# Value sums of an attention kernel in two runs per batch instead of three, under a new order of work

## Chip, cores and metric

The kernel runs on one core of a Trainium2 chip. The metric is the device time of one execution in microseconds (us), as the median of several runs. PE is the matrix engine (TensorE), DVE the vector engine, ACT the scalar engine, POOL GpSimd, SP the engine that issues most transfers.

## What is computed

Four batches (b = 0 to 3) of 1088 rows go through two blocks. The first is a linear attention with polynomial features, whose output is the input `x` of the second, an attention in which every row uses two of four experts:

```python
kv = np.einsum('bhsf,bhsd->bhfd', k_p, v)          # k_p, q_p: 64 features per head of k and q
num = np.einsum('bhsf,bhfd->bhsd', q_p, kv)        # block 1: x = num / den
logits = x @ w_gate                                # block 2: two experts per row
topk = np.argpartition(-logits, K, axis=-1)[..., :K]
for e in range(E):
    scores = scale * (q @ k.transpose(0, 2, 1))    # q, k, v = x @ wq[e], x @ wk[e], x @ wv[e]
    scores = np.where(causal, -1000000000.0, scores)
    a = softmax(scores)                            # row maximum, exp, division by the sum
    ye = a @ v @ wo[e]
    out += mask[..., None] * w[:, :, kk:kk + 1] * ye   # for each of the row's two choices kk
```

Everything is 32-bit floating point. `wq[e] @ wk[e].T` and `wv[e] @ wo[e]` are multiplied out once (`Mq`, `Mo`), so that the scores are taken against `x` itself and the "values" that are summed are rows of `x`.

## The kernel before

The 1088 rows of a batch are 17 **tiles** of 64 rows; each tile has 128 partitions, since each row appears once per chosen expert. The tiles lie in three **groups**: 0 to 5, 6 to 11, 12 to 16. The work is written as some 1290 **jobs**, each a short piece for one engine, with what it reads, makes and holds. A table of numbers, `ORDER`, says in which order they are recorded, and so in which order each engine, which runs its own queue in order, meets them; a letter behind a number picks one of two engines for a job, or, for an idle matmul, whether it is there (`a`) or not (`b`). Buffers come from pools, and a job's first use of one takes the one longest free.

For each batch the jobs are, by the names used below:

- **Block 1**: load k, q, v; `turn k`, `turn q` (DVE transpositions), `sketch` (PE, L524), `back` (DVE, L527, transposes the sketch out of PSUM), `features` (DVE or POOL, L532), `sums` (PE, L576: features of k against v), `numer` (PE, L635 and L771), `divide`, `turn x`, `keep x`, which give `xT`.
- **Choice of experts**: `logits` (PE, L829 and L822), `turn logits`, `choose`, masks `mb`. The gate's weights are a small transfer of their own (`load w4`, `wgr`), which POOL spreads (`gate order`, L294).
- **Per group**: `query` (PE, L1018: two pairs of products with `Mq`), `base` (copies) and `pick` (DVE, L1031, a predicated copy by the masks), which give `qs`.
- **Per tile**: `score` (PE, L1056), `take` (DVE, L1068: mask, minimum), `exp` (ACT, L1084), `guard`, `invert` (DVE, L1095), `weigh` (POOL, L1099), `turn A` (DVE, L1104: the weighed scores transposed, 32 by 32, into the buffer `AT`).
- **Per group**: the value sum `sum b.n` (PE, L1132) over all of the group's key blocks, `keep V` (copies by ACT or DVE), `patch V` (DVE, L1162), `spread V` (POOL, L1166), and `out` (PE, L1260, L1210 for the group of five tiles). The very last group of the kernel (batch 3, group 0) uses `mix V` (DVE, L1171) and `scale V` (POOL, L1175), and its `out` goes expert by expert (L1236).

A **value sum** walks over blocks j of 32 keys, `J = 2*t1` of them for a group that ends at tile `t1`. Each j has four matmuls (32 contracted rows each, in the four 32-row quarters of the array) that run side by side. They have 32 columns for each tile that sees these keys, so at most 192 for a group of six and 160 for one of five, and fewer, in steps of 32, on the group's own diagonal. The first matmul of a sum can start only when `turn A` of all tiles of its group is done. Its results lie in two of the four PSUM **pairs** (a pair is two banks of 512 columns) until `keep V` and `patch V` have read them.

PSUM has those four pairs for everything: scores, queries, sketches, sums, outputs. `AT` has two buffers, used in turn by the groups of all batches (12 group sums in the kernel). At the start PE also runs "dummy" matmuls on zeros (`idle`, L251), which nobody reads.

## Time and profile before

| | |
|---|---|
| median of 3 runs | 259.52 us (259.01 to 259.92) |
| span of the profiled execution | 258.5 us |
| difference of median and span (start and end of the program around it) | 1.0 us |
| PE busy | 249.4 us, 96% |
| DVE busy | 207.2 us, 80% |
| POOL busy | 157.8 us, 61% |
| ACT busy | 108.0 us, 42% |

The time of the profiled execution as such is not given apart from its span; sums are made against the span, and the 1.0 us is added at the end. "Busy" for PE is generous: matmuls are pipelined, and a short pause between two of them is hidden in the modelled end of the first. The pieces of the chain of waits, which follow each other without a gap, tell better what PE spent.

### The profile page before, as it was taken

How to read it: one execution, taken by the hardware profiler on the slowest of the kernel's cores; microseconds unless marked ns; L12 is line 12 of the kernel's file. 1: busy time of each engine (PE TensorE's matmuls, PEld its weight loads, DVE VectorE, ACT ScalarE, POOL GpSimd, SP SyncE). 2: the span in 40 equal slices, each digit the busy share in tenths (PEclk: the TensorE clock that was granted, in tenths of full speed). 3: DMA queues.
4: the chain of work that ended last, by engine and by line, in shares of the span. 5: the costliest groups of instructions: out<-in, count | busy, mean ns of one | idle time of the engine just before them, and what ended most of it. 6: DMA issues, size and time to landing. Idle time of an engine off the chain costs nothing.

```text
span 258.5 us, 9931 instructions
## 1 busy us (share of the span) xinstructions
PE 249.4 (96%) x4159; PEld 185.6 (72%) x4161; DVE 207.2 (80%) x527; ACT 108.0 (42%) x287; POOL 157.8 (61%) x265
## 2 busy tenths in 40 slices
PE   7888998999999999999999999999999999999995
PEld 2467654576598896665799776765896975789994
DVE  6969899998987886999997387999888638878332
ACT  4346445872803505840634044624624316432110
POOL 6718489958489754577663976087366634533742
PEclk9999999999999999999999999999999999999999
DMA  6936379205827552702612694304252157430003
GB/s 212 240 98 174 92 195 252 45 3 127 215 54 147 126 146 79 193 3 82 172 32 38 125 249 126 84 18 140 42 90 76 53 136 184 110 60 3 3 4 86
DMA packets 40381, 27.88 MB, mean 108 GB/s; under 512 B 25872, under 2 KB 35600, under 8 KB 40336
## 3 DMA queue, kind: packets, MB, share of 16 engines
q1 hardware_dynamic: 39888, 26.62, 42.8%
q8 instruction: 32, 0.52, 0.9%
q10 hardware_dynamic: 448, 0.62, 0.7%
q14 instruction: 13, 0.11, 0.1%
HBM read 22.62 MB, written 4.62 MB: 105 GB/s over the span
## 4 chain that ended last, share of the span: by engine, by line
PE 83%; DMA 6%; DVE 5%; POOL 2%; issue 2%; ACTq 0%; ACT 0%; DVEq 0%; POOLq 0%
PE pair L1132 30%; PE pair L1056 26%; PE pair L1018 9%; PE pair L1260 7%; PE pair L1210 3%; DMA wgr<-in_moe_w_gate_dram 2%; DMA w<-in_v_dram 2%; PE pair L771 2%; POOL fp L532 2%; DMA in<-in_q_dram 2%; PE pair L524 1%; PE pair L576 1%; DVE qs L1031 1%; PE pair L1236 1%; PE pair L822 1%
## 5 line engine op out<-in xcount | busy, mean ns | idle before, releaser
L1099 POOL TENSOR_SCALAR w<-w,rs,sh 128x960 f32<-128x960 f32 (+15 forms) x68 | 56.5, 837 | 32.1 <-DVE rs L1095 29.5
L1056 PE MATMUL pair<-xT,qs 128*128 128x320 f32 (+11 forms) x216 | 73.7, 478 | 1.3 <-DVE rs L1095 0.7
L1084 ACT ACTIVATE w<-w,mx 128x768 f32<-128x768 f32 (+16 forms) x68 | 52.3, 769 | 48.0 <-DVE mx L1068 44.3
L1068 DVE CUSTOM_DVE_ANT_0 w<-pair,mask 128x192 f32<-128x192 f32 (+14 forms) x68 | 48.3, 723 | 11.3 <-PE pair L1056 9.1
L1056 PEld LDWEIGHTS pair<-xT,qs 128*128 128x128 f32 x216 | 38.3, 190 | 26.5 <-issue 10.9
L1104 DVE STREAM_TRANSPOSE AT<-w 128x64 f32<-128x64 f32 (+15 forms) x68 | 50.7, 758 | 4.6 <-POOL w L1099 4.5
L1132 PE MATMUL pair<-AT,xra 32*128 32x160 f32 (+5 forms) x1136 | 44.6, 302 | 0.0
L1132 PEld LDWEIGHTS pair<-AT,xra 32*128 32x128 f32 x1136 | 41.8, 185 | 3.7 <-issue 1.5
L1166 POOL TENSOR_TENSOR agg<-agg,mb 128x768 f32<-128x768 f32 (+1 forms) x22 | 33.9, 1557 | 13.0 <-ACT agg L194 8.8
L1018 PE MATMUL pair<-xT,Mq 128*128 128x384 f32 (+1 forms) x96 | 34.3, 477 | 0.1
L194 ACT COPY agg<-pair 128x384 f32<-128x384 f32 (+1 forms) x34 | 14.1, 464 | 48.4 <-PE pair L1132 45.5
L532 POOL TENSOR_TENSOR fp<-w 128x576 f32<-128x576 f32 x22 | 26.6, 1223 | 2.8 <-DVE w L527 1.8
L1132 PE MATMUL pair<-AT,xrb 32*128 32x160 f32 (+5 forms) x752 | 27.2, 288 | 0.0
L1132 PEld LDWEIGHTS pair<-AT,xrb 32*128 32x128 f32 x752 | 26.3, 185 | 0.8 <-issue 0.7
L1031 DVE COPY_PREDICATED qs<-mb,pair 128x768 f32<-128x768 uint16 (+1 forms) x24 | 23.1, 964 | 2.6 <-DMA mb<-me 1.2
L1018 PEld LDWEIGHTS pair<-xT,Mq 128*128 128x128 f32 x96 | 17.3, 190 | 10.0 <-issue 2.1
L1260 PEld LDWEIGHTS pair<-Mo,agg 128*128 128x128 f32 x168 | 20.6, 192 | 3.2 <-issue 1.4
L1260 PE MATMUL pair<-Mo,agg 128*128 128x128 f32 x168 | 21.3, 277 | 0.0
L1092 POOL TENSOR_SCALAR rs<-zs 128x1 f32<-128x1 f32 x28 | 6.3, 226 | 20.8 <-ACT w L1084 17.9
L1162 DVE COPY_PREDICATED agg<-mb,pair 128x384 f32<-128x384 uint16 (+1 forms) x24 | 12.8, 554 | 6.5 <-ACT agg L194 6.3
L194 ACT COPY qs<-pair 128x384 f32<-128x384 f32 (+1 forms) x18 | 7.8, 459 | 16.4 <-PE pair L1018 16.4
L527 DVE STREAM_TRANSPOSE w<-pair 128x576 f32<-128x576 f32 x16 | 11.6, 755 | 3.2 <-PE pair L524 3.0
(173 smaller groups left out, 288.6 us busy)
## 6 DMA issues: line engine op xcount, KB each, us to landing
xra<-xd SPq DMA_DIRECT2D x16, 192.0 KB, 4.6
xrb<-xd SPq DMA_DIRECT2D x16, 192.0 KB, 4.8
xrc<-xd SPq DMA_DIRECT2D x16, 160.0 KB, 4.6
in<-in_k_dram SPq DMA_DIRECT2D x7, 272.0 KB, 4.4
mb<-me SPq DMA_DIRECT2D x3, 576.0 KB, 6.1
mb<-me SPq DMA_DIRECT2D x6, 288.0 KB, 3.9
in<-in_q_dram SPq DMA_DIRECT2D x3, 544.0 KB, 6.4
xd<-w SPq DMA_DIRECT2D x12, 136.0 KB, 3.1
```

Source lines behind the costliest of these rows:

```text
L194: (nc.scalar.copy if eng == "ACT" else VEC[eng].tensor_copy)(o, i)
L532: VEC[e].tensor_tensor(out=f, in0=a[:, :, None, R : 2 * R].to_broadcast([128, NJ, R, R]), in1=a[:, :, 0:R, None].to_broadcast([128, NJ, R, ...
L1018: nc.tensor.matmul(plan[ps[x]][:, y, 0:w], Mq[:, ((1, 2), (0, 3))[x][y]], plan[xT][:, 64 * t0 : 64 * t1], start=True, stop=True)
L1031: nc.vector.copy_predicated(chosen(), c, rows(plan[ps[x]]))
L1056: nc.tensor.matmul(plan[p][:, y, 0 : c1 - c0], plan[qs][:, 128 * t : 128 * t + 128], plan[xT][:, c0:c1], start=True, stop=True)
L1068: nc.vector.tensor_tensor_reduce(out=o, in0=src, in1=msk, scale=-1.0, scalar=mx[:, b, i, x - 1 : x] if x else 3e38, op0=ALU.add, op1=ALU.m ...
L1084: nc.scalar.activation(out=a, in_=a, func=ACTF.Exp, bias=mx[:, b, i, last : last + 1], scale=-1.0, accum_out=zs[:, b, i : i + 1])
L1099: nc.gpsimd.tensor_scalar(out=a, in0=a, scalar1=rs[:, b, i : i + 1], scalar2=plan[("sh", b)][:, i : i + 1], op0=ALU.mult, op1=ALU.mult)
L1104: nc.vector.transpose(dst[:, 0 : keys // 32, t], plan[A][:, 0:keys].rearrange("p (j s) -> p j s", s=32))
L1132: nc.tensor.matmul(plan[Vk[g // 2]][:, g % 2, lo : 32 * nt], plan[(f"xr{j // 12}", b)][rows, j % 12], a[rows, j, lo:], start=(j == 0), sto ...
L1166: nc.gpsimd.tensor_tensor(out=a, in0=a, in1=masks_in(plan[mb], w)[:, 2 * x : 2 * x + 2], op=ALU.mult)
L1260: nc.tensor.matmul(plan[p][0:m, 0, 128 * x : 128 * x + 128], plan[agg][:, e, 128 * x : 128 * x + m], Mo[:, e], start=(e == 0), stop=(e == ...
```

## The change

Groups 0 and 1 of a batch now share one value sum, over the tiles 0 to 11 (`sum b.01`), with up to 384 columns per key block; group 2 keeps its own. The turned scores therefore lie in two buffers of their own, `ATa` (tiles 0 to 11) and `ATb` (12 to 16), one of each instead of two of `AT`. `ATa` has two bands, for the key blocks that all twelve tiles may see (0 to 11) and for those that only the tiles 6 to 11 see (12 to 23), so `turn A` of the tiles 6 to 11 becomes two instructions. The jobs behind the sum (`keep V`, `patch V` and so on) stay per group and read their columns of the shared sums. In batch 3 the shared sum stands last, and both of its groups take the form of the last group (`mix V`, `scale V`, `out` by expert).

The core of the diff (the order is a table; a line of each side stands for it):

```diff
 ORDER = """
-1 3 0 2 48 76 77 4 74 51 37b 75 10a 60 46 52 84 50 81 54 49 88 8a 45 89 7a 17a 85 22a 78 80 97 86 79 53 87 400 98 100a
+1 12a 46 397 56 57 84 47 45 85 2 3 0 48 49 76 17b 4 77 23b 11b 25b 16b 6b 88 51 89 37b 39b 22b 36b 43b 28b 32b 40b 15b
...
-    atw = max(2 * t1 * (t1 - t0) * 32 for t0, t1 in groups)
+    value_groups = ((0, 1), (2,))
+
+    def turned_scores(b, n):
+        return ("ATa" if n < 2 else "ATb", b)
+
+    def bands(ns):
+        t0, t1 = groups[ns[0]][0], groups[ns[-1]][1]
+        at, out_ = 0, []
+        for n in ns:
+            j0, j1 = (0 if n == ns[0] else 2 * groups[n][0]), 2 * groups[n][1]
+            out_.append((j0, j1, groups[n][0], at))
+            at += (j1 - j0) * (t1 - groups[n][0]) * 32
+        return out_, at
+
+    def band_of(b, n):
+        return next(ns for ns in value_groups if n in ns)
...
-        "AT": several("AT", 2, [128, atw]),
+        "ATa": several("ATa", 1, [128, bands((0, 1))[1]]),
+        "ATb": several("ATb", 1, [128, bands((2,))[1]]),
...
         def turn():
-            dst = plan[AT][:, 0 : 2 * t1 * nt * 32].rearrange("p (j t s) -> p j t s", t=nt, s=32)
-            nc.vector.transpose(dst[:, 0 : keys // 32, t], plan[A][:, 0:keys].rearrange("p (j s) -> p j s", s=32))
+            for j0, j1, a0, at in bands(band_of(b, n))[0]:
+                nt, j1 = groups[band_of(b, n)[-1]][1] - a0, min(j1, keys // 32)
+                if j0 < j1:
+                    dst = plan[AT][:, at : at + (j1 - j0) * nt * 32].rearrange("p (j t s) -> p j t s", t=nt, s=32)
+                    nc.vector.transpose(dst[:, :, i - a0], plan[A][:, 32 * j0 : 32 * j1].rearrange("p (j s) -> p j s", s=32))
...
+    def summed(b, n):
+        ns = band_of(b, n)
+        return ("V", b, ns[-1]), [("ps", "V", b, ns[-1], l) for l in range(2)], groups[n][0] - groups[ns[0]][0]
+
+    def sum_values(b, ns, rank):
+        v = ns[-1]
+        t0, t1 = groups[ns[0]][0], groups[v][1]
+        nt = t1 - t0
+        AT = turned_scores(b, v)
+        made, Vk, _ = summed(b, v)
+        J = 2 * t1
...
+        def block(j0, j1):
+            for j in range(j0, j1):
+                b0, _, a0, at = [x for x in bands(ns)[0] if x[0] <= j][-1]
+                m = 32 * (t1 - a0)
+                a = plan[AT][:, at + (j - b0) * m : at + (j - b0) * m + m]
+                for g in range(4):
+                    rows, lo = slice(32 * g, 32 * g + 32), first(j, g % 2)
+                    if lo < 32 * nt:
+                        nc.tensor.matmul(plan[Vk[g // 2]][:, g % 2, lo : 32 * nt], plan[(f"xr{j // 12}", b)][rows, j % 12],
+                                         a[rows, lo - 32 * (a0 - t0) :], start=(j == 0), stop=(j == J - 2 + g % 2))
...
     def last_group(b, n):
-        return b == B - 1 and n == 0
+        return b == B - 1 and n < 2
...
+            ns = band_of(b, n)
+            if n == (ns[0] if b == B - 1 else ns[-1]):
+                sum_values(b, ns, vt)
             values(b, n, vt)
```

The order has more in it than the sums. It has 12 dummies instead of 8, nine of them ahead of the first sketch (five before). It issues the gate's weights as the first transfer of all, the loads of k of batch 1 earlier, and it moves two of the `features` of q and k from DVE to POOL.

PE around the first value sum of batch 0. Before, the sum of group 0 stands alone behind the `logits` and `sums` of the next batches (L822, L576):

```order
L1056 MATMUL pair_64<-xT_85,qs_97 128x448
L1056 MATMUL pair_63<-xT_85,qs_97 128x352 x2
L1056 MATMUL pair_66<-xT_85,qs_97 128x512
L1056 MATMUL pair_65<-xT_85,qs_98 128x416 x2
L822 MATMUL pair_64<-xT_86,wg 32x288 x4
L576 MATMUL pair_66<-vp_71,fp_79 32x33 x72
L1132 MATMUL pair_63<-AT_100,xra_87 128x192 x2
L1132 MATMUL pair_64<-AT_100,xra_87 128x192 x2
```

Now (new line numbers: L1074 score, L840 logits, L542 sketch, L1159 value sum) the shared sum is the first one, behind the scores of tiles 12 and 15:

```order
L1074 MATMUL pair_64<-xT_85,qs_98 128x416
L840 MATMUL pair_66<-xT_86,wg 32x288 x4
L542 MATMUL pair_63<-in_67,SKk 32x288 x8
L542 MATMUL pair_65<-in_67,SKk 32x288 x8
L1074 MATMUL pair_64<-xT_85,qs_98 128x416
L1074 MATMUL pair_66<-xT_85,qs_98 128x512 x2
L1159 MATMUL pair_65<-ATa_99,xra_87 128x384 x2
L1159 MATMUL pair_63<-ATa_99,xra_87 128x384 x2
```

The three-microsecond sum of group 0 is gone from its place, and the first L1159 waits for twelve tiles instead of six.

DVE in the opening, from the last sketches of k of batch 0 to the first `divide`. Before, all six of DVE's remaining `features` (L532) stand in a row, and the two `turn k` of batch 1 (L490) behind them, then a copy and the two `back` of its sketch (L527):

```order
L527 STREAM_TRANSPOSE w_77<-pair_63 128x576
L532 TENSOR_TENSOR fp_78<-w_76 128x9x64
L532 TENSOR_TENSOR fp_79<-w_77 128x9x64 x4
L490 STREAM_TRANSPOSE in_69<-in_67 128x544 x2
L194 COPY kvz_81<-pair_63 64x2x33
L527 STREAM_TRANSPOSE w_75<-pair_64 128x576
L527 STREAM_TRANSPOSE w_75<-pair_65 128x576
L642 TENSOR_SCALAR den<-pair_63 128x12
```

Now (L550 features, L508 turn k, L512 turn q, L545 back, L660 divide):

```order
L545 STREAM_TRANSPOSE w_77<-pair_64 128x576
L550 TENSOR_TENSOR fp_79<-w_77 128x9x64
L508 STREAM_TRANSPOSE in_67<-in_68 128x544
L550 TENSOR_TENSOR fp_79<-w_77 128x9x64
L508 STREAM_TRANSPOSE in_67<-in_68 128x544
L512 STREAM_TRANSPOSE in_68<-in_69 128x576
L512 STREAM_TRANSPOSE in_68<-in_69 128x512
L545 STREAM_TRANSPOSE w_74<-pair_66 128x576
L545 STREAM_TRANSPOSE w_74<-pair_65 128x576
L660 TENSOR_SCALAR den<-pair_64 128x12
```

The two `turn q` of batch 1 now stand between its `turn k` and its `back`; before they stood behind the `divide` jobs.

DVE at the end of the kernel, behind the last value sum. Before, two `mix V` (L1171) and two `patch V` (L1162), then the transposition of `out 3.2` (L1213) and the final copies:

```order
L1171 TENSOR_TENSOR agg_102<-pair_63,mb_95 128x2x6x32
L1162 COPY_PREDICATED agg_102<-mb_95,pair_63 128x2x6x32
L1171 TENSOR_TENSOR agg_102<-pair_66,mb_95 128x2x6x32
L1162 COPY_PREDICATED agg_102<-mb_95,pair_66 128x2x6x32
L1213 STREAM_TRANSPOSE ob_103<-pair_65 128x320
L194 COPY ob_104<-pair_64 128x128 x2
```

Now both groups' work stands there (L212 copy, L1196 patch, L1205 mix, L1209 scale, L1247 transposition of `out 3.2`):

```order
L212 COPY agg_102<-pair_65 128x2x6x32
L1196 COPY_PREDICATED agg_102<-mb_93,pair_63 128x2x6x32
L1205 TENSOR_TENSOR agg_102<-pair_63,mb_93 128x2x6x32
L1196 COPY_PREDICATED agg_102<-mb_93,pair_65 128x2x6x32
L1247 STREAM_TRANSPOSE ob_103<-pair_64 128x320
L1205 TENSOR_TENSOR agg_102<-pair_65,mb_93 128x2x6x32
L1209 TENSOR_TENSOR agg_102<-agg_102,mb_93 128x384
L1196 COPY_PREDICATED agg_101<-mb_95,pair_63 128x2x6x32
L1205 TENSOR_TENSOR agg_101<-pair_65,mb_95 128x2x6x32
L1196 COPY_PREDICATED agg_101<-mb_95,pair_65 128x2x6x32
L1205 TENSOR_TENSOR agg_101<-pair_63,mb_95 128x2x6x32
```

Five DVE instructions behind the last sum became eleven, and the one on which the first `out 3.0` rests is the last of them.

## Rows read from the trace of the kernel before

**Rows 1.** The page: granted clock of TensorE in tenths, 40 slices of the span

```profile
PEclk9999999999999999999999999999999999999999
```

**Rows 2.** Busy us in a stretch of the opening: span, PE, PEld, DVE, ACT, POOL, clock, DMA, GB/s

```profile
30.00:40.00 10.00, 9.39 (x95) 5.41 (x96) 9.72 (x36) 5.62 (x19) 7.81 (x22) 1.00 0.63 169
```

**Rows 3.** Busy us by stretch, same columns, from PE's saturation on

```profile
42.45:59.95 17.50, 17.47 (x363) 11.85 (x364) 16.35 (x51) 11.35 (x27) 13.18 (x22) 1.00 0.33 62
59.95:243.00 183.05, 183.05 (x2855) 139.89 (x2857) 148.92 (x354) 72.54 (x199) 111.88 (x167) 1.00 0.42 102
```

**Rows 4.** The chain of waits in order of time: start us, us, what (matmul halves)

```profile
42.45 1.24 PE pair L1056 x4
...
54.60 1.26 PE pair L576 x133
55.85 3.14 PE pair L1132 x81
...
59.25 6.86 PE pair L1056 x18
...
70.41 7.01 PE pair L1132 x174
...
120.90 0.65 PE pair L1018 x2
```

**Rows 5.** Matmuls of the first sums by shape: busy us, mean ns, idle before

```profile
L1132 PE MATMUL pair<-AT,xra 32*128 32x128 f32 x16 | 1.0, 270 | 0.0
...
L1132 PE MATMUL pair<-AT,xra 32*128 32x32 f32 x16 | 1.0, 264 | 0.0
```

**Rows 6.** Timeline of DVE: start us, us, instructions [idle before, and its end]

```profile
11.35 3.73 DVE L532 TENSOR_TENSOR fp<-w 128x576 f32<-128x576 f32 x5
16.16 1.37 DVE L490 STREAM_TRANSPOSE in<-in 128x544 f32<-128x544 f32 x2 [1.08 <-DMA in<-in_k_dram]
...
18.72 1.45 DVE L527 STREAM_TRANSPOSE w<-pair 128x576 f32<-128x576 f32 x2 [0.93 <-PE pair L524]
```

**Rows 7.** The same timeline later: logits, the picks of groups 0 and 1

```profile
26.62 0.38 DVE L833 STREAM_TRANSPOSE ch<-pair 128x192 f32<-128x192 f32 x1 [0.38 <-PE pair L829]
...
30.98 2.17 DVE L1031 COPY_PREDICATED qs<-mb,pair 128x768 f32<-128x768 uint16 x2
...
40.13 1.36 DVE L749 STREAM_TRANSPOSE fp<-fp 128x1152 f32<-128x1152 f32 x1
41.42 0.97 DVE L1031 COPY_PREDICATED qs<-mb,pair 128x768 f32<-128x768 uint16 x1
```

**Rows 8.** Timeline of POOL at the start, same columns

```profile
8.76 2.81 POOL L532 TENSOR_TENSOR fp<-w 128x576 f32<-128x576 f32 x2 [1.76 <-DVE w L527]
```

**Rows 9.** Timeline of SP: start us, us of issuing, transfer

```profile
0.79 0.39 SPq L237 DMA_DIRECT2D w<-in_S_dram  x1
...
10.79 1.73 SPq L271 DMA_DIRECT2D wgr<-in_moe_w_gate_dram  x1
```

**Rows 10.** The page's groups: line, engine, operation, count | busy us, mean ns | idle before

```profile
L1068 DVE CUSTOM_DVE_ANT_0 w<-pair,mask 128x192 f32<-128x192 f32 (+14 forms) x68 | 48.3, 723 | 11.3 <-PE pair L1056 9.1
...
L1104 DVE STREAM_TRANSPOSE AT<-w 128x64 f32<-128x64 f32 (+15 forms) x68 | 50.7, 758 | 4.6 <-POOL w L1099 4.5
```

**Rows 11.** Timeline of all engines behind the last value sum, same columns

```profile
250.27 2.42 PE L1210 MATMUL pair<-agg,Mo 128*128 128x320 f32 x8
250.41 0.56 DVE L1171 TENSOR_TENSOR agg<-pair,mb 128x384 f32<-128x384 f32 x1 [3.93 <-PE pair L1132]
...
251.74 0.91 POOL L1175 TENSOR_TENSOR agg<-agg,mb 128x384 f32<-128x384 f32 x1 [2.40 <-DVE agg L1162]
...
252.53 2.84 PE L1236 MATMUL pair<-Mo,agg 128*128 128x128 f32 x24
```

**Rows 12.** Timeline of PE at the start, same columns

```profile
1.24 3.73 PE L251 MATMUL pair<-idle 128*128 128x512 bf16 x10 [1.24 <-DVE idle L244]
5.55 2.24 PE L524 MATMUL pair<-w,SK 32*32 32x288 f32 x68 [0.58 <-DVE w L494]
```

More of the change, by code (lines that the diff above doesn't have):

```diff
@@ L252 @@
             ["idle"], None, [h], mode="F", rank=-190 + 0.01 * x)
-    raws = ("AT", "weights")
+    raws = ("ATb", "weights")
     def weight(x):
@@ L950, in fetch_masks @@
             nc.sync.dma_start(out=plan[("mb", b, n)][:, 0 : 384 * (t1 - t0)], in_=src.partition_broadcast(128))
-        onehot = ("AT", "weights")
+        onehot = ("ATb", "weights")
         def widen_masks(x, t):
@@ L1111, in scores, with first, cost @@
             ("a", b, i), [A, ("sh", b)], rank=rank)
-        job(f"turn A {b}.{i}", "DVE", keys * 0.001035 + 0.18, lambda e: turn(), [("a", b, i)], ("AT", b, n), [A, AT], rank=rank)
+        job(f"turn A {b}.{i}", "DVE", keys * 0.001035 + 0.18, lambda e: turn(), [("a", b, i)], AT, [A, AT], rank=rank)
+    def summed(b, n):
[8 more added lines that the diff above has]
+        J = 2 * t1
+        def first(j, h):
+            return 32 * max(0, j // 2 - t0) + (32 if j % 2 and j // 2 >= t0 and h == 0 else 0)
+        def block(j0, j1):
[8 more added lines that the diff above has]
+                                         a[rows, lo - 32 * (a0 - t0) :], start=(j == 0), stop=(j == J - 2 + g % 2))
+        def cost(j0, j1):
+            return sum(max(2 * (32 * nt - first(j, 1)) / 1200, 0.105 if j == J - 1 else 0.21) + 0.005 for j in range(j0, j1))
+        for j0 in range(0, J, 4):
+            j1 = min(j0 + 4, J)
+            need = [AT, ("xr", b, j0 // 12)] + ([(*made, j0)] if j0 else [])
+            job(f"sum {b}.{''.join(map(str, ns))}.{j0}", "PE", cost(j0, j1), lambda e, j0=j0, j1=j1: block(j0, j1), need,
+                (*made, j1) if j1 < J else made,
+                [AT, *Vk, (f"xr{j0 // 12}", b)], mode="V", rank=rank + 0.001 * j0)
     def values(b, n, rank):
@@ L1117, in values @@
         w = 64 * nt
[L1118 to L1143 removed]
+        agg, mb = ("agg", b, n), ("mb", b, n)
+        made, Vk, shift = summed(b, n)
         def by_half(a):
@@ L1155, in sums_of @@
         def sums_of(l):
-            return plan[Vk[l]][:, :, 0 : 32 * nt].rearrange("p h (t s) -> p h t s", s=32)
+            return plan[Vk[l]][:, :, 32 * shift : 32 * shift + 32 * nt].rearrange("p h (t s) -> p h t s", s=32)
         def keep(e, x):
```

126 lines of the change are left out of this document (53 added, 73 removed).

## Prediction

> **What bounds the kernel now.** I read first the busy time by stretch, then the chain of waits, then the timelines of single engines. The granted clock stands at its upper mark in every slice [rows 1], so idle matmuls have no clock left to win. Two regimes follow each other. In the opening DVE is the limit: from 30 to 40 us it works 9.72 of 10 us [rows 2]. From 42.45 us on PE works without a pause, 17.47 of 17.50 us and then 183.05 of 183.05 [rows 3], and the chain of waits is a list of PE pieces that touch each other [rows 4]. So from 42.45 us to the tail every microsecond taken from PE's list comes off the end, and one taken from another engine is worth nothing, unless PE comes to wait for it. In the opening a microsecond counts if it lets DVE's list end sooner. Behind the last value sum a short chain of several engines counts.
>
> **A. The sums: PE's work shrinks.** Two sums of batch 0 stand in the chain: group 0 takes 3.14 us, group 1 takes 7.01 [rows 4]. Group 0 has 12 key blocks of 192 columns, less its diagonal: per matmul quarter 2 x (192+160+128+96+64+32) = 1344 columns. Group 1 has 12 full blocks more, 3648. A line through both has a slope of (7.01-3.14)/2304 = 1.68 ns a column and starts at 0.88 us. A third row agrees on the slope: the two query pieces of 384 columns took 0.65 us [rows 4], 1.69 ns a column. So a sum costs 0.88 us whatever its columns, and rows say where it sits: a matmul of 32 columns takes as long as one of 128, 264 against 270 ns [rows 5], so the narrow end of the diagonal is paid as if it were wide.
> The shared sum walks 24 blocks with the same 4992 columns, but pays one narrow diagonal instead of two: 4992 x 1.69 + 0.84 = 9.28 us against 10.15. That is 0.87 us a batch, **-3.5 us** for four. Ends: -2.3, if a third of the 0.88 us turns out to be the fill of the array and stays, and -3.9, if the wider matmuls run a little better than the line. (A price per block instead of one per sum would fit both sums too, at 0.76 ns a column and 0.18 us a block, and would save 2.1 us a batch; the query row, at 1.69 ns, excludes it.)
> The Trainium skill, "TensorEngine Tiling (Array Packing)", section "Instruction Overhead", puts the floor of a matmul at about 60 columns. By that only the two 32-column blocks of a diagonal are padded, by 28 columns each, and the four merges would save an estimated 0.4 us (4 x 2 x 28 x 1.69 ns). The equal times at 32 and 128 columns speak against it here.
>
> **B. The opening: when PE may start its first shared sum.** The first value sum of before could start after six tiles; now it needs twelve. What counts is how much of PE's list is done by then. In the new order everything that PE did up to 54.60 us, and the score piece of 6.86 us [rows 4] less tile 13, lies ahead of the first shared sum. Tile 13 has 896 columns, 1.51 us at 1.69 ns. So before stood at the same progress at 54.60 + 6.86 - 1.51 = 59.95 us. The question is whether the new opening gets there sooner, and DVE decides it, with twelve tiles to mask and turn.
> - To the second pick of group 0, which ended at 33.15 us [rows 7]. Ahead of it DVE waits three times: 1.08 us for k of batch 1, 0.93 for its sketch [rows 6], 0.38 for the logits [rows 7], 2.39 in all. Now k is loaded earlier and `turn q` stands between `turn k` and `back`, so I take the waits as filled. Two features leave for POOL and one moves behind the pick, 3 x 3.73/5 [rows 6] = -2.2; two `turn k` of batch 2 (1.37 [rows 6]), two copies and a base (three of about 0.56, the nearest row being a 384-column operation [rows 11]) come ahead of it, +3.05. With small ones that drop out I take +0.4 net. The gate's weights are now issued ahead of S; the issue of S itself took 0.39 us, that of the gate's weights 1.73 where they stood [rows 9]: I take +0.4. Together 33.15 - 2.39 + 0.4 + 0.4 = 31.6.
> - To the first pick of group 1: 42.39 - 33.15 = 9.24 us before [rows 7], now without the two `turn k`, 7.8. That is 39.4.
> - To the last `turn A` of tile 11: nine takes (0.723), nine turns (0.758 [rows 10]), two picks (0.97), two `turn f` (1.36 [rows 7]), two `back` (0.73 [rows 6]), the logits (0.38 [rows 7]) and small reciprocals (0.9): 20.7 us. Each starts some 0.06 us before the end of the one ahead of it (40.13 + 1.36 against 41.42 [rows 7]); 34 of them, -2.0; the second half of the turns of tiles 6 to 11, +0.6. That is 19.3, and the sum starts at 58.7.
> So **-1.2 us**. Ends: -3, if DVE also loses the short pauses behind the picks, and +1.5, if its waits stay and the gate's load costs its 1.73. The two features that POOL takes cost 1.4 us each there [rows 8], with POOL idle 1.76 us ahead of them; their users stand later, so I count nothing.
>
> **C. PSUM.** A shared sum holds two of the four pairs until twelve tiles are copied and patched, where a group's sum held them for six: seven DVE operations of about 0.56 us [rows 11] beside ACT's copies, 3.5 to 4 us instead of 2. PE's work that needs no more than the other two pairs behind it is tile 13 (1.5), the `sums` piece (1.26) and a query piece (two of 0.65) [rows 4], about 4 us. Cover and hold are nearly equal. I take 0.2 a batch, **+0.8 us**; ends 0 and 6.
>
> **D. The tail.** Before, from the end of the last sum to the end of PE: 250.27 to 252.53 + 2.84 = 255.37, 5.1 us [rows 11], with no pause on PE. Group 1's output, another 2.84, lay earlier, so this work was 7.95 us. Now both outputs stand behind the last sum, and the first `out 3.0` needs the last of eleven DVE operations, 11 x 0.55 = 6.0 us, then its own 2.84: 8.9. **+1.0 us**; ends 0.3 (DVE's overlaps of 0.06 each) and 1.5 (POOL's scale of 0.91 [rows 11] still on the path).
>
> **Idle matmuls: 0.** A dummy is two matmuls, and ten took 3.73 us [rows 12]; nine dummies end near 1 + 18 x 0.37 = 7.7 us as matmul halves are shown, about 6.5 by their starts. The sketch had to wait for DVE's `turn` even before (5.55 us, idle 0.58 [rows 12]), and now it waits for q's, near 6.5. What is left is inside B's bounds.
>
> **The sum.** 258.5 - 3.5 - 1.2 + 0.8 + 1.0 = 255.6 us of span, and with the 1.0 us around it **256.6 us**, to compare with the median of 259.52.
>
> **Rivals.**
> - *DVE never waits* (13%). The waits in front of the picks go and so do those behind, B gives -3 and C nothing: 254 to 255. For it: the three waits are each a plain matter of one late input. Against it: the first sum now rests on the whole DVE list of twelve tiles.
> - *The gate* (17%). The opening's waits stay, since k, the sketch and the logits come no sooner than DVE gets to them: the pick stays at 33.2, the sum starts at 60.3, PE waits there, B is +0.4, and C costs 1.5 to 2: about 259.1, no difference. For it: DVE is full at 9.7 of 10 whatever is moved.
> - *PE stands at the shared sums* (18%), the slower one. Behind each shared sum PE soon needs a third pair while two are held; DVE's keeps and patches stand in one queue with the takes that free the score pairs, so both come late. It decides where PE's pair-free work behind the sum is shorter than the hold of 3.5 us. With DVE a take and a turn late (0.72 + 0.76 [rows 10]), some 1.3 to 2 us stay open in each batch: +5 to +8 instead of +0.8, and 260.8 to 263.8. For it: PE has no slack anywhere [rows 3], so each such pause is the kernel's. Against it: DVE has some 34 us free of 183 [rows 3].
> The Trainium skill speaks for this rival: "TensorEngine Tiling (Array Packing)", section "PSUM Bottleneck", says that tiling speeds up the matmuls and not the emptying of PSUM, which may become the limit. The trace of before cannot show it, with no pause on PE.
> - *The merge saves little* (5%). If the 0.88 us hangs on the columns that each group brings and not on a diagonal of its own, the shared sum pays it twice, 4992 x 1.69 ns + 1.75 = 10.2 us, A gives nothing, and 260.1 comes out. The equal times in [rows 5] and the line through two sums speak against it.
> By the floor of the Trainium skill, "TensorEngine Tiling (Array Packing)", "Instruction Overhead", A would be the estimated 0.4 us, and the end 259.7.
>
> **How the numbers follow.** My forecast has 47%, 254.9 to 258.3 by itself. A measurement of this kernel tells about 0.3%, 0.8 us, from no change: below 258.74 is faster, above 260.30 slower. Faster: the forecast, *DVE never waits* and a little of *the gate*, 0.62. Same: most of *the gate* and *saves little*, 0.18. Slower: PSUM and what lies above *the gate*, 0.20. The range leaves out a strip on each side: below, the less likely part of *DVE never waits* goes, above, the part of *PE stands* beyond 262, some 15% together: 254.0 to 262.0.
>
> **What would show it.** A: shared sums of batch 0 of 9.0 to 9.6 us in the chain. B: the second pick of group 0 ending near 31.6, the first shared sum starting near 58.7, and DVE without pauses before it. C: PE's pauses behind shared sums of under 0.5 us each. D: 8.5 to 9 us from the end of the last sum to the end of PE. The prediction is wrong if PE's pauses between 59 and 250 us come to more than 2 us, if a shared sum takes over 9.8, or if the first one starts after 60 us.

## The result: 1.2% slower, and the profile after

The changed kernel takes 262.78 us in the median of four runs (262.07 to 263.65), against 259.54 us of the kernel before on the same chip (259.01 to 259.92). The ratio is 1.0124, with a 95% interval of 1.0082 to 1.0165. The forecast was 256.6 us with a range of 254.0 to 262.0, so the time is above the range, on the other side of no change. The profiled execution has a span of 261.5 us, 3.0 more than before.

The page of the changed kernel, busy time of the engines and the granted clock in slices of a fortieth of the span:

```profile
PE 249.0 (95%) x3800; PEld 181.9 (70%) x3801; DVE 215.9 (83%) x562; ACT 106.9 (41%) x274; POOL 160.3 (61%) x269
...
PEclk9999999999999999999999999999999999999999
```

The clock is at its upper level throughout, as in [rows 1]. PE is busy as long as before, although 3.5 us of matmul work are gone: four idle jobs have come, and these are generous sums, so the places have to be looked at one by one. First the shared sums. The chain of waits of the changed kernel, in order of time (start us, us, what):

```profile
120.00 9.25 PE pair L1159 x173
...
152.30 8.98 PE pair L1159 x267
...
175.88 9.25 PE pair L1159 x172
...
230.95 18.32 PE pair L1159 x411
249.27 2.37 PE pair L1244 x8
```

A shared sum takes 9.25 us (the 8.98 are group 2's own sum, and the last row holds both, 9.34 + 8.98). Before, the two sums took 3.14 and 7.01 [rows 4]. Four times 0.9 us are saved, as forecast. So the loss lies elsewhere, and the timeline of PE shows where it stands still (start us, us, instructions [idle before, and its end]):

```profile
52.10 0.71 PE L789 MATMUL pair<-fp,kvr 32*32 32x288 f32 x6 [0.20 <-DMA kvr<-kd]
53.32 1.51 PE L789 MATMUL pair<-fp,kvr 32*32 32x256 f32 x58 [0.51 <-DMA kvr<-kd]
...
62.58 6.23 PE L1159 MATMUL pair<-ATa,xra 32*128 32x384 f32 x94 [0.24 <-DVE ATa L1125]
...
76.12 1.56 PE L1036 MATMUL pair<-xT,Mq 128*128 128x384 f32 x4 [0.96 <-ACT kvs L212]
...
78.35 0.78 PE L542 MATMUL pair<-in,skx 32*32 32x288 f32 x32 [0.30 <-DVE ATb L1125]
...
88.60 3.71 PE L1074 MATMUL pair<-xT,qs 128*128 128x288 f32 x12 [0.66 <-DVE qs L1049]
131.83 0.25 PE L594 MATMUL pair<-vp,fp 128*32 128x33 f32 x3 [1.26 <-issue]
252.23 2.63 PE L1270 MATMUL pair<-Mo,agg 128*128 128x128 f32 x20 [0.17 <-DVE ob L1247]
255.16 3.17 PE L1270 MATMUL pair<-Mo,agg 128*128 128x128 f32 x24 [0.30 <-DVE agg L1205]
```

Before, PE had no pause between 42.45 us and the end of the last sum [rows 3]. Now the first shared sum starts at 62.58 us, where the kernel before stood at the same progress at 59.95 us: 2.6 us late. Behind it PE loses 0.96 + 0.30 + 0.66 + 1.26 = 3.2 us. The tail, from 249.27 us to PE's end at 258.13 by the chain of waits, is 8.9 us, 0.9 more than before. In all -3.5 + 2.6 + 3.2 + 0.9 = +3.2, against 3.0 in the spans.

**Why the first sum is late.** The timeline of DVE in the opening, same columns:

```profile
2.77 1.13 DVE L327 TENSOR_SCALAR w<-w 16x32 int32<-16x32 int32 x1 [1.51 <-DMA w<-in_S_dram]
...
3.94 0.17 DVE L330 TENSOR_SCALAR w<-w 16x32 int32<-16x32 int32 x1
...
15.37 0.74 DVE L508 STREAM_TRANSPOSE in<-in 128x544 f32<-128x544 f32 x1 [0.29 <-DMA in<-in_k_dram]
...
19.12 1.37 DVE L512 STREAM_TRANSPOSE in<-in 128x576 f32<-128x576 f32 x2 [1.71 <-DMA in<-in_q_dram]
...
32.34 2.15 DVE L1049 COPY_PREDICATED qs<-mb,pair 128x768 f32<-128x768 uint16 x2 [0.17 <-ACT mb L212]
```

Three things are in it. The decode of S, whose instructions otherwise take 0.17 us each, stands for 1 us at its start, until POOL has finished a large fill; the timeline of POOL:

```profile
2.92 0.95 POOL L305 MEMSET mask<- 128x1024 bf16 x1
```

The wait for k and its sketch [rows 6] has gone, but a wait of 1.71 us for q of batch 1 has come, since `turn q` now stands ahead of `back`. And the loads of `kvr` of batch 1, which PE's `numer` needs at 52 us, are issued by SP at 45.10 to 48.66, behind transfers of v of batch 2 and of `xra`.

**Why PE stops behind the first sum.** The chain of waits there:

```profile
72.73 0.93 DVE ATb L1125
73.65 0.45 DVE agg L212
74.24 3.25 POOL agg L1200 x2
77.67 3.22 POOL agg L1200 x2
...
81.77 4.52 DMA mb<-me
86.41 1.04 DVE qs L1049
87.54 1.02 DVE qs L1049
88.60 3.71 PE pair L1074 x12
```

This chain is a matter of buffers in SBUF, and not of PSUM. There are three mask buffers `mb`. The masks of groups 0 and 1 are wanted last by POOL's `spread V` (L1200). Group 0's used to come free after its own sum; its first successor was loaded from 64.88 us on. Now both are held until twelve tiles are summed, copied and spread, and only then does the load of the next batch's mask start, 4.5 us long, with the picks and PE's scores behind it. DVE comes late to its copies as well, because three operations right behind the sum's start are stretched:

```profile
63.13 1.19 DVE L876 TENSOR_TENSOR ch<-ch 128x9 f32<-128x9 f32 x1
...
64.32 1.17 DVE L878 TENSOR_TENSOR ch<-ch 128x18 f32<-128x18 f32 x1
...
65.51 1.74 DVE L550 TENSOR_TENSOR fp<-w 128x576 f32<-128x576 f32 x1
```

The same L876 and L878 took 0.16 and 0.17 us at 28 us, and L550 0.72 at 16 us. Beside them POOL runs three `features` in a row, some 1.17 us each:

```profile
63.11 3.52 POOL L550 TENSOR_TENSOR fp<-w 128x576 f32<-128x576 f32 x3
```

The first two stretched operations end as one of those does (64.32 and 65.49), and the third ends 0.6 us behind the last, which is about its own length. The Trainium skill, "SBUF — State Buffer", section "SBUF: two separate sides", says that DVE and GpSimd share a pair of ports under an exclusive lock, which an operation of DVE with two SBUF inputs needs against an operation of GpSimd that reads SBUF; whoever comes second stands for the whole instruction. The stretches agree with it.

Two pauses stand ahead of this one, 0.96 and 0.30 us, and the first of them is a wait for PSUM all the same. Timelines of ACT and DVE:

```profile
75.84 0.23 ACT L212 COPY kvs<-pair 128x66 f32<-128x66 f32 x1
78.13 0.17 ACT L212 COPY skx<-pair 128x8 f32<-128x8 f32 x1 [2.06 <-PE pair L735]
...
76.06 1.05 DVE L1196 COPY_PREDICATED agg<-mb,pair 128x384 f32<-128x384 uint16 x2
...
78.23 1.05 DVE L1086 CUSTOM_DVE_ANT_0 w<-pair,mask 128x896 f32<-128x896 f32 x1
```

By the program's order the `query` at 76.12 us writes the same pair as the `sums` of batch 2 before it, and ACT's copy at 75.84 empties this pair. The other three are held: two by the shared sum, until the last `patch V` ends at 77.1, and one by the scores of tile 13, which `take` reads from 78.23 on. PE's work behind the sum had lasted 3.3 us (71.83 to 75.16), and the sum's pairs are held for 5.3. The pause of 0.30 ends with ACT's copy of `skx` at 78.30 (the `turn A` that its row names ends at the same time, and in f4 the row names the copy). That copy waits for a small matmul (L735), whose input POOL makes at 77.44, between the spreads of the two groups. Neither of the two sets when the scores at 88.60 start, since these wait for the picks anyhow: in e2, where the pause of 0.96 is gone, PE waits 0.68 there.

### The profile page after: what moved, and what is told of

The parts are those of the page before. It is cut to its first block, busy times and chain, and to the rows that moved or that the text cites. A ratio compares the mean times of both kernels' runs of the same rounds, so it can differ in the third digit from the quotient of the medians.

```text
span 261.5 us, 9219 instructions
## 1 busy us (share of the span) xinstructions
PE 249.0 (95%) x3800; PEld 181.9 (70%) x3801; DVE 215.9 (83%) x562; ACT 106.9 (41%) x274; POOL 160.3 (61%) x269
## 4 chain that ended last, share of the span: by engine, by line
PE 64%; DVE 14%; DMA 12%; POOL 6%; issue 2%; SPq 0%; ACT 0%; DVEq 0%; POOLq 0%; ACTq 0%
PE pair L1159 24%; PE pair L1074 20%; PE pair L1036 6%; PE pair L1294 5%; PE pair L1244 3%; DMA in<-in_q_dram 3%; DMA xra<-xd 3%; POOL agg L1200 2%; DMA in<-in_k_dram 2%; DMA kvr<-kd 2%; DMA mb<-me 2%; PE pair L789 2%; DVE w L545 1%; DVE w L1086 1%; PE pair L1270 1%
## 5 line engine op out<-in xcount | busy, mean ns | idle before, releaser
L1102 ACT ACTIVATE w<-w,mx 128x512 f32<-128x512 f32 (+15 forms) x68 | 52.5, 773 | 64.6 <-DVE mx L1086 48.6
L1117 POOL TENSOR_SCALAR w<-w,rs,sh 128x320 f32<-128x320 f32 (+14 forms) x68 | 56.7, 838 | 29.7 <-DVE rs L1113 27.9
L1074 PE MATMUL pair<-xT,qs 128*128 128x384 f32 (+11 forms) x216 | 73.4, 478 | 1.0 <-DVE qs L1049 1.0
L1074 PEld LDWEIGHTS pair<-xT,qs 128*128 128x128 f32 x216 | 38.2, 190 | 26.3 <-issue 10.1
L1086 DVE CUSTOM_DVE_ANT_0 w<-pair,mask 128x768 f32<-128x768 f32 (+15 forms) x68 | 48.2, 726 | 4.2 <-PE pair L1074 3.0
L1200 POOL TENSOR_TENSOR agg<-agg,mb 128x768 f32<-128x768 f32 (+1 forms) x20 | 30.7, 1555 | 12.4 <-ACT agg L212 6.0
L550 POOL TENSOR_TENSOR fp<-w 128x576 f32<-128x576 f32 x26 | 31.7, 1237 | 3.1 <-DVE w L545 2.6
L1125 DVE STREAM_TRANSPOSE ATa<-w 128x384 f32<-128x384 f32 (+5 forms) x72 | 28.8, 440 | 1.9 <-POOL w L1117 1.8
L1159 PE MATMUL pair<-ATa,xra 32*128 32x320 f32 (+6 forms) x384 | 26.1, 412 | 0.2 <-DVE ATa L1125 0.2
L212 ACT COPY agg<-pair 128x384 f32<-128x384 f32 (+1 forms) x28 | 11.4, 470 | 35.3 <-PE pair L1159 31.1
L1159 PEld LDWEIGHTS pair<-ATa,xra 32*128 32x128 f32 x384 | 23.1, 185 | 3.8 <-DVE ATa L1125 1.7
L1125 DVE STREAM_TRANSPOSE ATb<-w 128x832 f32<-128x832 f32 (+4 forms) x20 | 23.1, 1163 | 0.0
L212 DVE COPY agg<-pair 128x384 f32<-128x384 f32 (+1 forms) x16 | 7.9, 521 | 15.0 <-PE pair L1159 13.5
L1159 PEld LDWEIGHTS pair<-ATb,xra 32*128 32x128 f32 x384 | 13.4, 185 | 1.8 <-issue 0.7
L1159 PE MATMUL pair<-ATb,xra 32*128 32x160 f32 x384 | 14.4, 298 | 0.0
L1196 DVE COPY_PREDICATED agg<-mb,pair 128x384 f32<-128x384 uint16 (+1 forms) x24 | 12.8, 555 | 1.7 <-ACT agg L212 1.4
```

Of the source, the lines that this page charges most:

```text
L212: (nc.scalar.copy if eng == "ACT" else VEC[eng].tensor_copy)(o, i)
L550: VEC[e].tensor_tensor(out=f, in0=a[:, :, None, R : 2 * R].to_broadcast([128, NJ, R, R]), in1=a[:, :, 0:R, None].to_broadcast([128, NJ, R, ...
L1074: nc.tensor.matmul(plan[p][:, y, 0 : c1 - c0], plan[qs][:, 128 * t : 128 * t + 128], plan[xT][:, c0:c1], start=True, stop=True)
L1086: nc.vector.tensor_tensor_reduce(out=o, in0=src, in1=msk, scale=-1.0, scalar=mx[:, b, i, x - 1 : x] if x else 3e38, op0=ALU.add, op1=ALU.m ...
L1102: nc.scalar.activation(out=a, in_=a, func=ACTF.Exp, bias=mx[:, b, i, last : last + 1], scale=-1.0, accum_out=zs[:, b, i : i + 1])
L1117: nc.gpsimd.tensor_scalar(out=a, in0=a, scalar1=rs[:, b, i : i + 1], scalar2=plan[("sh", b)][:, i : i + 1], op0=ALU.mult, op1=ALU.mult)
```

## Experiments

In each diff the numbers are jobs of the table `ORDER` of the changed kernel; a letter behind an idle job's number (two matmuls) says that it is there (`a`) or not (`b`). The edits of e1 and f3 are told in words. Ratios are against the kernel before on the same chip in the same series (259.67 us in the series of e1 to e4, 259.9 in f1 to f4, 259.15 in g1 to g3).

**The merge alone.** The order is that of the kernel before, except for what the merge forces; the tail is the changed one.

```diff
-sum b.0                        at its place behind six tiles
-sum b.1, out b.0, out b.1      at their places
+sum b.01                       at the place of sum b.1
+out b.0                        at the place of out b.1
+out b.1                        behind sum b.2
```

> The order of the kernel before, with only the sums merged: the shared sum stands where the sum of group 1 stood (in batch 3 where the last sum stood, with the changed kernel's tail behind it), what hangs on group 0's sum follows as soon as its buffers allow, the outputs of group 0 take the places of those of group 1, and these go behind the sum of group 2. Theory 1 (the merge is good by itself, and the new order of the opening lost the gain): the sums give -3.5 us, the tail +0.9, and some waits +1 to +2, so 257 to 259 us. Theory 2 (the merge has a price of its own, since the masks and the two PSUM pairs of groups 0 and 1 are held until the shared sum is patched, and the next batch's masks, queries and scores wait for them): PE stands 3 us or more behind each of the first three shared sums, 265 to 285 us.

It takes 329.07 us, ratio 1.268 (1.259 to 1.277), far above the 265 to 285 us of its second theory. The sums themselves are as in the changed kernel (9.34 us). Its waits, summed (us, times, longest):

```profile
DVE qs L1049 <- DMA mb<-me: 20.9, 3, 8.2
PE pair L1074 <- DVE qs L1049: 11.7, 3, 8.8
```

Its chain of waits behind the first sum:

```profile
66.48 9.34 PE pair L1159 x173
75.84 0.57 DVE agg L212
76.43 0.87 ACT agg L212 x2
77.30 0.07 issue
77.37 3.25 POOL agg L1200 x2
80.64 4.26 DMA mb<-me
...
84.99 1.02 DVE qs L1049
```

So the mask chain is what a merge costs first of all: sum, copies, spread, load, pick, with PE idle for 8.68, 8.78 and 10.46 us behind the first three shared sums, 28 of the 69 us. With PE standing, the granted clock falls as well (0.91 over the execution, single slices at 0.5 to 0.8), and that adds to the loss. The new order of the changed kernel is thus no extra beside the merge. It buys back all but 3 of the 69 us.

**POOL's weigh ahead of its features.** Two jobs of tile 14 of batch 0 move ahead of the three `features` that stretch DVE.

```diff
-985 703a 705a 704a 344 345 360
+985 344 345 703a 705a 704a 360
```

> The changed kernel with one job moved on POOL: weigh of tile 14 goes ahead of the three features of k of batch 2 (63.1 us on). Theory 1 (DVE's operations with two inputs from SBUF stand while POOL works on features): the choose operations and DVE's own feature, which took 0.48 to 1.74 us, take 0.2 and 0.75, DVE is 2 to 3 us ahead at the take of tile 12 (64.3 instead of 67.2 us), PE's waits at 78.4 (0.30) and 88.6 us (0.66) shrink, and the end is 0.5 to 1.0 us earlier, near 262.0. Theory 2 (what sets PE at 88.6 us is the masks of batch 1, which wait for POOL's spreads and a load of 4.5 us): DVE is ahead, but the pick stays at 86.4 us and the end within 0.4 us of 262.8.

262.37 us, 1.0105 (1.005 to 1.016), against the changed kernel no difference that can be told. DVE's take comes 1.1 us sooner and the pause of 0.96 is gone, but two operations are still stretched (L878, 0.98, beside the weigh, and L550, 1.74, beside the first feature) and PE waits 0.68 for the pick at 87.82. The chain behind the sum is now the mask chain without a gap, 9.36, ACT 1.25, POOL 3.25 and 3.22, load 4.66, picks. Taking part of DVE's delay away uncovers the buffers.

**The loads of kvr earlier.**

```diff
-136 686 688 685 135 137 144 419 418 139 417 140 420 141
+136 419 418 417 420 686 688 685 135 137 144 139 140 141
```

> The changed kernel with four jobs moved on SP: the loads kvr<-kd of batch 1 stand right behind the store of kd, ahead of the loads of v of batch 2. Theory 1 (the first shared sum is late by the queue of SP too: numer of batch 1 waited 0.2 and 0.5 us for kvr, and DVE 0.97 us for the scores behind it): no wait at numer, first shared sum near 61.7 instead of 62.6 us, end 0.7 to 1.0 us earlier, near 261.9. Theory 2 (DVE's list alone sets the first sum): DVE has no pause at 55 us but the sum starts at 62.3 or later, and the end is within 0.4 us of 262.8.

262.11 us, 1.0074 (1.0044 to 1.0104). The pauses of 0.20 and 0.51 are gone, and the first sum starts at 60.79 instead of 62.58. Not all of that is the edit's: the load of q, issued as before, left DVE waiting 0.50 us here, and 0.85 to 1.71 in the runs in which the opening is the changed kernel's own (e2, f3, g1 as far as the wait for q, g3 and after). In those the first sum starts between 61.67 and 62.71. Counted from the start of DVE's `back` of k of batch 1, it comes 41.2 us later here and 41.7 to 42.9 in those five, so the edit is worth 0.4 to 1.7 us of the sum's start.

**The load of q earlier.**

```diff
-389 388 55 391 390 394
+389 388 390 55 391 394
```

> The changed kernel with one job moved on SP: the load of q of batch 1 goes ahead of the last weights (wo) and of v. Theory 1 (DVE's wait of 1.71 us for q of batch 1 delays all that follows): q lands near 18.1 instead of 19.05 us, the second pick of group 0 ends near 33.6 instead of 34.5, the first shared sum starts 0.9 us earlier, and the end is 0.5 to 0.9 us earlier. Theory 2 (the wait only passes on, to the sketch of k behind it, which PE had at 19.2 us): the back of k moves by less than 0.3 us, and the end is within 0.4 us of 262.8.

262.69 us, 1.0145 (1.0069 to 1.0221): the time decides nothing. In the trace DVE's wait of 1.71 us is replaced by one of 0.62 for the sketch, and the first sum starts at 61.48, 0.2 us ahead of the earliest of those five. A part of the gain waits elsewhere.

**Both moves.** The two diffs above together.

> The changed kernel with both moves on SP: kvr of batch 1 ahead of v of batch 2, and q of batch 1 ahead of the last weights. Alone the first brought the first shared sum from 62.6 to 60.8 us, the second to 61.5. Theory 1 (two waits on one chain add up): the first shared sum starts near 59.9, and the end is 2 to 2.5 us earlier than the changed kernel's, near 260.5. Theory 2 (DVE's list of twelve tiles takes over): it starts at 60.5 or later, and the end is that of the first move alone, near 261.8.

262.07 us, 1.008 (1.0049 to 1.0112), first sum at 61.08, no sooner than with the first move alone: the gains do not add. With both inputs early DVE's list of twelve tiles is the limit, as PE's wait at the first sum says (0.43 us for `ATa`, the last turn).

**Fewer idle matmuls at the start.** Four of the nine ahead of the first sketch are off.

```diff
-34a 27a 83a 29a 13a
+34b 27b 83a 29b 13b
```

> The changed kernel with four of its nine idle jobs ahead of the first sketch left out (eight matmuls), nothing else. In the changed kernel, and in the three runs made from it by moving a job, PE stands 1.3 to 1.8 us two or three matmuls before the end of the same piece (sums of batch 3, about 130 us), and the trace names no releaser. Theory 1 (it is a place in PE's instruction stream, where code has not come yet): with 16 instructions fewer ahead, the place falls behind that piece, among long score matmuls, the pause goes, and the end is 1.0 to 1.5 us earlier, near 261.5 us. Theory 2 (it is a semaphore that the trace does not show): the pause stays at the same matmuls. Either way the opening moves by less than 0.3 us if idle matmuls are hidden behind DVE's decode and turns.

262.64 us, 1.0097 (1.0061 to 1.0134). The busy time by stretch (span, PE, PEld, DVE, ACT, POOL, clock, DMA, GB/s):

```profile
7.00:9.60 2.60, 2.28 (x67) 1.42 (x65) 2.29 (x4) 0.00 (x0) 0.49 (x3) 0.93 1.13 195
9.60:13.00 3.40, 3.40 (x69) 2.01 (x69) 2.84 (x7) 0.91 (x3) 2.86 (x3) 0.50 1.15 276
13.00:17.00 4.00, 3.78 (x18) 2.37 (x17) 3.97 (x6) 1.42 (x3) 3.21 (x2) 0.61 1.03 231
```

PE had stood for 0.72 and 0.32 us ahead of the sketches, and from 9.6 to 13 us the granted clock is 0.50, the level of 1.2 GHz, where the changed kernel has 1.00. A sketch piece of 64 matmuls, which takes 1.73 us in the changed kernel, takes 2.62 there, and the first sum starts at 63.32, 0.7 us later than in the changed kernel and 0.6 to 1.7 later than in the five runs named under e3. So in this opening the extra idle matmuls are worth some 0.6 us or more. They cover a sketch that comes late. The pause of 1.26 us at 131 us is gone, as the first theory had it; the gain of 1.0 to 1.5 us that it expected from this is largely lost in the opening.

**POOL's spread given to DVE** for group 1 of batch 0.

```diff
-spread V 0.1.*   POOL
+spread V 0.1.*   DVE
```

> The changed kernel with the two spreads of group 1 of batch 0 done by DVE instead of POOL. Theory 1 (behind the first shared sum PE waits at 88.6 us for a chain of copies, four spreads on POOL in a row, the load of the masks into a buffer that the spreads held, and two picks): the masks of group 1 of batch 1 land 1.5 to 2 us earlier, near 84.5 instead of 86.3 us, PE's wait of 0.66 at 88.6 us goes, and the end is 0.5 to 0.7 us earlier. Theory 2 (it is DVE that is late there): DVE's 1.8 us more keep the wait at 0.6 us or make it longer, and the end is the same or later.

263.46 us, 1.0136 (1.0076 to 1.0196). The two spreads take 1.80 us on DVE (3.2 on POOL), but the take behind them is late and PE waits 1.14 us for it; the last of the picks starts at 87.64, where it started at 87.54. DVE has no room at this place.

**The opening repaired.** Both moves of loads, the gate's weights back to a later place, POOL's fill of the mask (job 47) behind its copies of SK, and the four idle matmuls off.

```diff
-12a 46 397 56 57 84 47 45 85
+12a 46 397 84 45 85
...
-78 59 53
+78 59 47 53
...
-64 44a 393
+64 44a 56 393
...
-93b 94b 399
+93b 94b 57 399
```

> The changed kernel with the opening put right: both moves on SP, the long memset of the mask on POOL behind the copies of the sketch's matrix as before, the gate's weights loaded late as before, and four idle jobs less. Theory 1 (the opening lost by the order of the loads and by POOL's long memset beside DVE's decode, and the rest of the loss is the stall at 130 us): first sketch at 5.6 to 6.0 instead of 7.0 us, first shared sum near 58.8 instead of 62.6, no stall at 130 us: 3.7 + 1.3 us, less 1 that comes back as a longer wait for the masks of batch 1, the end near 258.8, level with the kernel before or a little faster. Theory 2 (the merge's own waits behind the shared sum eat what the opening gives): PE's waits between 70 and 92 us grow by 2 us or more, and the end stays over 260.5.

259.35 us, 0.9951 (0.9915 to 0.9987). Timelines of DVE and PE at the start:

```profile
2.58 0.17 DVE L327 TENSOR_SCALAR w<-w 16x32 int32<-16x32 int32 x1 [1.32 <-DMA w<-in_S_dram]
...
5.62 2.73 PE L542 MATMUL pair<-w,SK 32*32 32x288 f32 x64
```

and PE from the first sum on:

```profile
59.82 6.23 PE L1159 MATMUL pair<-ATa,xra 32*128 32x384 f32 x94 [0.42 <-DVE ATa L1125]
73.37 1.56 PE L1036 MATMUL pair<-xT,Mq 128*128 128x384 f32 x4 [0.97 <-ACT kvs L212]
75.59 0.78 PE L542 MATMUL pair<-in,skx 32*32 32x288 f32 x32 [0.30 <-ACT skx L212]
```

The decode runs at full speed with POOL's fill and its spreading of the gate's weights elsewhere, the first sketch starts at 5.62 us instead of 7.01 with fewer idle matmuls and the clock at 1.00 (nothing stands ahead of the sketch now), and the first sum starts at 59.82 (58.8 expected). Two pauses of the first batch are left, 0.97 and 0.30. The pauses at 88 and 131 us are gone, though the chain of waits still runs through the masks. PE ends at 253.61 by the timeline, 4.7 us before the changed kernel (258.33); 1.7 us of that are missing from the span of this execution (258.5), because it ends 4.2 us after ACT's last issue of an output, against 2.5. It is the one version of this study that is measured faster than the kernel before, by half a per cent.

**Fewer idle matmuls later.** Three other idle jobs off, 12 instructions of PE in all (six matmuls and their weight loads); the start is the changed kernel's.

```diff
-64 44a 393 392 91 100a 101b 102b 38a 21a 92
+64 44b 393 392 91 100a 101b 102b 38b 21b 92
```

> The changed kernel without its three later idle jobs (the six matmuls at 9 to 13 us; the nine jobs ahead of the first sketch stay). It asks again after the pause of 1.3 us near 130 us, which was gone when four of the early idle jobs were left out, but there the granted clock also fell to 0.50 and 0.61 from 9.6 to 17 us and the opening was 0.7 us later. Theory 1 (the pause belongs to a place in PE's instruction stream): with 12 instructions fewer ahead it is gone here too, the opening moves by less than 0.4 us, and the end is 0.8 to 1.3 us earlier than the changed kernel's, near 261.7. Theory 2 (it went because the opening moved): the pause is there, at the same matmuls, and the end within 0.4 us of 262.8.

261.31 us, 1.0073 (1.0034 to 1.0111). The clock stays at 1.00, and PE at the place of the pause reads:

```profile
127.67 1.43 PE L594 MATMUL pair<-vp,fp 128*32 128x33 f32 x144
129.03 1.55 PE L1074 MATMUL pair<-xT,qs 128*128 128x512 f32 x3
130.82 1.23 PE L1074 MATMUL pair<-xT,qs 128*128 128x512 f32 x3 [0.23 <-issue]
```

Of 1.26 us 0.23 are left. The three idle jobs would be over long before, and no engine's wait ends there. What changed is how many instructions PE has had by then. The pause stands in all seven kernels in which PE has as many as in the changed one (that one, e2, e3, e4, f2, f3, g3: 1.2 to 1.8 us), and in none of the four with 12 to 16 fewer (f1, f4, g1, g2) but for g1's 0.23. In the seven traces it stands behind PE's 2131st to 2133rd matmul, and g1's 0.23 behind its 2132nd, which is there six matmuls further in the program. So the pause goes with the count of PE's instructions, as the first theory has it, and not with a piece of work.

**DVE's choice later.** The choice of batch 1 (the stretched operations) and one `features` behind the next take and a transposition.

```diff
-348 460 702b 347 296 297 298 299 325 462 326 327a 441 461
+348 347 296 297 298 299 325 326 327a 441 460 702b 462 461
```

> The changed kernel with the first of these two moves alone: choose, maximum and feature on DVE behind its transposition of x. Theory 1 (operations of DVE with two inputs from SBUF stand while POOL works): the eight that took 0.18 to 1.74 us from 62.6 us on take 0.2, and 0.75 for the feature; DVE's copies of the shared sum start at 72.0 to 72.5 instead of 73.57 us, the pick of group 1 at 85.0 to 85.5 instead of 86.41, PE's wait of 0.66 us at 88.6 us shrinks to under 0.3, and the end is 0.3 to 0.7 us earlier than the changed kernel's. Theory 2 (the same operations are slow wherever they stand): they take 1 us again behind the transposition, and the copies start at 73.5.

262.19 us, 1.0106 (1.0056 to 1.0155). L875 and L878 are still stretched (1.22 and 1.06), now beside the last of POOL's features and its weigh. The pause of 0.96 falls to 0.27, and 0.68 us stand at 88.30, for the masks. The delay goes where POOL is, and the mask chain sets that point anyhow.

**The repaired opening with the late choice** and ACT's copy of the sums of batch 2 ahead of its copies of the shared sum.

```diff
+348 347 296 ... 441 460 702b 462 461
-363 230a 229b
+363 230a 708a 229b
```

> The repaired kernel (259.35 us, 0.5% under the kernel before) with two more moves behind the first shared sum: DVE's choose, maximum and feature of the next batches stand behind its transposition of x (so that no operation with two inputs from SBUF meets POOL's three features), and ACT's copy of the sums of batch 2 ahead of three of its copies of the shared sum. Theory 1 (each of these two waits is on the chain behind the shared sum): DVE's copies of the shared sum start within 0.6 us of its end instead of 1.8, PE's wait of 0.97 us for the copy of the sums goes, the masks of group 1 and the picks come 1.2 us earlier, and the end is 1.0 us earlier, near 258.3, 0.9% under the kernel before. Theory 2 (one wait passes on to the next, as in the kernel with weigh moved): PE's waits from 70 to 90 us add up to 1 us again, and the end is 259 or later.

258.85 us, 1.0001 (0.9976 to 1.0027). The wait for ACT's copy is gone, and in its place PE waits 0.96 us one step on, for an operation of POOL that stands behind its spreads of group 0 (L720, `zx`): one wait passes on to the next, as the second theory had it. Level with the kernel before, and with f4 as far as two series can tell: 0.9951 and 1.0001 have different runs of before under them, 259.9 and 259.15.

## Why the prediction was wrong, step by step

| step | forecast, us | measured, us |
|---|---|---|
| A, the sums | -3.5 | -3.5 |
| B, start of the first shared sum | -1.2 | +2.6 |
| C, PE behind the shared sums | +0.8 | +3.2 |
| D, the tail | +1.0 | +0.9 |
| sum of span | -2.9 | +3.2 (spans: +3.0) |

**A was right** in mechanism and size: 9.25 to 9.34 us a sum, 9.28 forecast. That fits the diagonal of its own as the thing saved. The rival *the merge saves little* is out.

**D was right**: 8.9 us as forecast, in the order forecast.

**B failed** at the sentence "I take the waits as filled". Moved instructions filled the wait for k and the sketch, but one of those moved (`turn q`) waits for a load of its own: 0.29 + 1.71 + 0.17 = 2.17 us of waits stand ahead of the second pick, where 2.39 stood before. The start was under-priced too: 0.4 us were set aside for the gate's weights, and the first sketch came 1.46 later, because S landed later by 0.2, the decode stood beside POOL's fill, and what follows on DVE moved on with it. The second pick ended at 34.49 us (31.6 forecast). The pick at 41.42 [rows 7], which the forecast took for the first of group 1, is its second; the first stands ahead of it in the timeline of before, and the second of the changed kernel is the last line here:

```profile
39.23 1.00 DVE L1031 COPY_PREDICATED qs<-mb,pair 128x768 f32<-128x768 uint16 x1
...
41.91 1.01 DVE L1049 COPY_PREDICATED qs<-mb,pair 128x768 f32<-128x768 uint16 x1
```

To this second pick it took 8.4 us (7.8 forecast), and from there to the last turn 19.7 (19.3), with PE and then DVE waiting through the late `kvr` (0.71 and 0.97 us), which the prediction did not follow through SP's queue. So 2.9 of the 3.9 us by which the sum came later than forecast were lost ahead of the second pick of group 0. f4 shows that these causes together are the right ones: with them mended the sum starts at 59.82, 2.8 us sooner than in the changed kernel and 1.9 to 2.9 sooner than in the five runs named under e3. It also shows that the forecast of 58.7 was too good even so; *the gate*, the rival that had the sum start at 60.3 since DVE is full, describes the mended opening.

**C failed in mechanism.** The step that failed is "Cover and hold are nearly equal", and with it the choice to ask about PSUM alone. In the first batch the cover was 3.3 us instead of about 4, since the `query` piece that was counted into it needs a third pair, and the hold was 5.3 instead of 3.5 to 4; PE stood for 0.96 us, until the pair of the `sums` was empty. So the rival *PE stands at the shared sums* was right in the mechanism of this one pause, but not in its size or in its 1.3 to 2 us in each batch, and that 262.78 lies in its 260.8 to 263.8 us is luck. The other pauses have other releasers: a copy that hangs on POOL's spreads (0.30), the mask buffers (0.66), and a place in PE's instruction stream (1.26), which no step of the prediction contains. Three of the four stand in the first batch and one in the second, none in the others. The prediction looked at what the merge holds longer in PSUM, and did not ask what else is held until a sum has been spread. e1 puts that hold beyond doubt, with 20.9 us of waits for the masks. How long the pairs would make PE wait if the masks did not has not been separated: a fourth mask buffer, which would do it, was not tried.

**Idle matmuls** were put at 0 on the ground that the clock has nothing to win [rows 1]. f1 shows that the clock would have been lost with fewer of them, some 0.6 us or more of the sum's start. They hold the first sketch back too (they end near 7.0, and the first half of q was turned at 6.40), but its second half waits for DVE until 7.41 anyway in f1. On the other side, their number moves PE's later instructions: with three jobs fewer, in a place where the clock does not need them, g1 has lost the pause of 1.26 us, and its ratio is 1.0073 against 1.0124 (the intervals overlap).

**Around the span** the prediction had 1.0 us. The runs list time and span, which differ by about 1.7 us in nearly all of them (263.26 and 261.5 for the profiled one of after). The profiled execution of before was thus itself some 0.7 us above the median of its kernel. To get from its span to a median the 1.0 us is right, so the miss does not hang on it.

**The range** ended at 262.0, with the upper 1.8 us of the slow rival cut off. The loss in B and that in C are two mechanisms, and the prediction never let both of them come true together.

## What to carry to other kernels

Merging two accumulations saved here what the trace's line through two sizes says (9.25 to 9.34 us a sum, 9.28 forecast), but it also lengthens every hold that ended with the first of them: list all buffers that are released behind it (here the masks, and in one place a pair of PSUM), follow each to its next load, and price that chain. When an instruction is moved into another's wait, ask for its own inputs, and look up where their loads stand in the issuing queue. And price what runs beside it on POOL, since a short operation of DVE beside a long one of POOL took up to 1.2 us here instead of 0.17.
